# A chain of casting and adding GpSimd transfers ahead of a GEGLU kernel, and in its down stage

## Chip, cores and metric

One core of one Trainium2 chip. The metric is device time in microseconds (us), from launch to end on that core. Every time below is such a time or a time inside one profiled execution, counted from its first instruction.

## What is computed

The reference, cut to what matters:

```python
def reference(x, w_gate, w_up, w_down):       # x (32, 32, 1024); w_gate, w_up (1024, 3584); w_down (3584, 1024); all bf16
    return (gelu_tanh(x @ w_gate) * (x @ w_up)) @ w_down
```

With the two leading axes of x taken together it is a feed-forward layer on N = 1024 rows: two products of 1024 x 1024 by 1024 x 3584, a gated product of the two, and a product of 1024 x 3584 by 3584 x 1024.

## The kernel before

**Two stages.** The gate/up stage makes `hT`, the transposed gated product (28 blocks of 128 features, 1024 columns, bf16). The down stage multiplies it by w_down. Both use a seven-product scheme for two-by-two blocks in place of eight block products: sums and differences of operand blocks are formed first, products of these are made, and the results are combined. The sums are held in `S` (20 slots of 128 x 512, `F32R`) and `T` (eight units of 2 x 4 x 128 per partition, `F32R`); the down stage sees the same memory of `T` as 16 slots, `T2r`.

**Start.** The first columns of x come in through two plain loads into `xn` (a part of `hT`), one on SP's queue and one on ACT's. PE transposes them with the identity `ident`, which GpSimd (POOL) makes with a `memset` and an `affine_select`. Ahead of that PE runs eight warm-up matmuls on a constant. The rest of x comes through transposing transfers on SP's queue. The weight blocks of the first pairs are loaded by `load_quad`, on SP's queue and on ACT's, behind the two x loads.

**Gate/up.** Pairs p = 0 to 13 take feature blocks p and p + 14. `sums_w` makes the weight sums of a pair, some on DVE, some on POOL, one on ACT. The sums of x are in `S`; the last pair reads slots 12 to 15 in its product 3 and slots 16 to 19 in its product 4.

**Down.** `sweep` runs the products in the order 1, 2, 7, 5, 6, 3, 4. K is cut into NK = 14 blocks for each half. For products 7, 5 and 6 the first operand is made by `prep7`, `prep5` and `prep6`, two blocks of k at a time, into slots of `S` by

```python
s_at = lambda b, k: 2 * ((b * 7 + k // 2) % 10) + k % 2
hs = lambda b, k: S[:, s_at(b, k):s_at(b, k) + 2, :]
```

with b = 0 for product 7, 1 for product 5, 2 for product 6. So product 5 uses slots 14, 16, 18, 0, 2, 4, 6 (each with its neighbour) for k = 0, 2, ..., 12, and the last four pairs are those that product 7 read for k = 0, 2, 4, 6. `prep6` reads what `prep5` made. In `sweep` the first `EDGE` = 4 blocks of k run for three of the four row tiles and then for the fourth; the middle blocks run k by k over all four; the last four blocks run tile by tile.

**Order.** `_Program.add` records every operation with its engine and, from the memory cells that it reads and writes, the operations that it has to wait for; `after` adds more of these. `finish` sorts each engine's operations by a due time `at` and then by the order of recording; PE keeps the order of recording. `at` sorts only: no operation waits for it. `emit` issues each engine's list in order, with a wait on a semaphore ahead of an operation where one is needed, so an operation that waits holds up everything behind it on its engine, transfers included. All operations are issued in `emit`, so nearly all of them have one line in the profile, L117.

Of the kernel before, what the change touches and what calls it, by code (L numbers as in the profile page):

```python
# [6 lines left out]
P = 128  # L7
BF16 = mybir.dt.bfloat16
FP32 = mybir.dt.float32
F32R = mybir.dt.float32r  # L10
ACTF = mybir.ActivationFunctionType
ALU = mybir.AluOpType
# [111 lines left out]
def bass_standalone__geglu_ffn__sampling_kernel(  # L124
# [15 lines left out]
    x_r = xf.rearrange("(tc p) d -> p tc d", p=P)  # L140
    w_r = [w.rearrange("(dk p) f -> p dk f", p=P) for w in (w_gate, w_up)]
    wd_r = w_down.rearrange("(m p) d -> p m d", p=P)

    pr = _Program()

    with ExitStack() as es:
        def sb(name, shape, dtype):
            return es.enter_context(nc.sbuf_tensor(name, shape, dtype))

        hT = sb("hT", [P, FM, N], BF16)  # L150
        arena = sb("arena", [P, 28672], BF16)
        S = sb("S", [P, 20, 512], F32R)
        T = sb("T", [P, 8, 2, 4, P], F32R)
# [12 lines left out]
        xn = hT[:, FM - 1, :].rearrange("p (t c) -> p t c", c=2 * P)  # L166
        Sf = S[:, :, :].bitcast(FP32)
# [15 lines left out]
        def tt(out, a, b, op, at, eng="dve", after=()):  # L183
            return pr.add(eng, "tensor_tensor", out, a, b, op, at=at, after=after)
# [4 lines left out]
        def dma(eng, out, a, at, name, after=()):  # L189
            return pr.add(eng, "dma_start", out, a, at=at, dma=name, after=after)  # L190

        GELU, COPY = ACTF.Gelu_apprx_tanh, ACTF.Copy
        ADD, SUB, MUL = ALU.add, ALU.subtract, ALU.mult


        one = nc.const_aps.tensor(1.0, [P, 512], BF16)
        pr.add("pool", "memset", ident[:, :], 0.0)
        pr.add("pool", "affine_select", ident[:, :], ident[:, :], [[-1, P]], ALU.not_equal, 1.0,
# [3 lines left out]

        NX = 2
        for i, eng in enumerate(("sp", "act")):
            dma(eng, xn[:, 2 * i:2 * i + 2, :], x_r[:, 2 * i:2 * i + 2, 0:NX * P], 0, f"xn{i}")

        def load_quad(eng, q, j, k0, k1, at=0, after=()):
            dma(eng, quad[q][:, j, k0:k1, :], w_r[j][:, k0:k1, 4 * q * P:4 * (q + 1) * P], at, f"w{q}_{j}_{k0}", after)
# [81 lines left out]
        for m in (0, 2):  # L290
            at = 21.9 + 2.59 * m
# [76 lines left out]
        for p in range(8, EARLY):  # L368
            at = 18.9 + (p - 4) * 3.46
            g = (2, 0)[p - 8]  # L370
            u = g + 1
# [21 lines left out]
        for p in range(NP):  # L393
            t0 = T0[p]
            short, last = p < EARLY, p == NP - 1
# [9 lines left out]
            at = lambda s: t0 + s * SLOT  # L405
# [27 lines left out]
            o = 4 if short else 7.8 if last else 5.9  # L433
# [58 lines left out]
        def hb(i, j, k):  # L492
            m = (KL if j == 0 else KR)[k]
            return hT[:, m:m + 2, i * 512:(i + 1) * 512]
# [5 lines left out]
        def wb(i, j, k): return wd[i][j][:, k:k + 2, :]  # L500
# [5 lines left out]
        hs = lambda b, k: S[:, s_at(b, k):s_at(b, k) + 2, :]  # L506
# [52 lines left out]
        clock = base + 1.5  # L559
        V = 1.22  # L560
# [3 lines left out]
            tt(ws(0, k), wb(1, 1, k), wb(0, 1, k), SUB, clock + V * (7 + k / 2))  # L564

        def prep5(k):
            tt(hs(1, k), hb(1, 0, k), hb(1, 1, k), ADD, clock + V * (14 + k))
            tt(ws(1, k), wb(0, 1, k), wb(0, 0, k), SUB, clock + V * (15 + k))

        def prep6(k):  # L570
# [23 lines left out]
        one_w = lambda b: (lambda k: T2r[:, t_at(b, k), :])  # L594
        sweep(7, PA, True, one_t(0), one_w(0), lambda t, at: act(p7[t], bank(PA[t]), COPY, at), prep7)
        sweep(5, PA, True, one_t(1), one_w(1), lambda t, at: act(p5[t], bank(PA[t]), COPY, at), prep5)
        sweep(6, PB, False, one_t(2), one_w(2), lambda t, at: act(bank(PA[t]), bank(PB[t]), COPY, at), prep6)
        for t in range(4):
# [48 lines left out]
```

## Time and profile before

| what | value |
|---|---|
| median of the runs shown | 271.56 us (271.51 and 271.62) |
| span of the profiled execution | 270.8 us; 0.7 to 0.8 us of a run's time lie around it |
| PE (matmuls) busy | 268.2 us, 99% |
| PEld (weight loads) busy | 192.6 us, 71% |
| DVE busy | 208.2 us, 77% |
| ACT busy | 136.1 us, 50% |
| POOL busy | 37.1 us, 14% |
| mean granted TensorE clock | 1.000 |
| first x loads issued | 0.73 and 0.74 us |
| products 7, 5 and 6 of the down stage | 202.1 to 240.4 us |

PE is TensorE's matmul, PEld its weight load, which overlaps with it; DVE is VectorE, ACT ScalarE, POOL GpSimd, SP SyncE. A queue such as SPq is where that engine issues transfers. A line of the timeline has a start, a duration, the engine, the operation with its output and input, and a count; the part in brackets is idle time before it and what ended it. The kernel before issues no transfer from POOL: all of its own go through SP's and ACT's queues.

### The profile page before, as it was taken

The page shows a single profiled execution, that of the slowest core. Times are in us where ns is not written, and L with a number is a line of the kernel's source. Part 1 is how long each engine was busy: PE and PEld are TensorE (multiplying, and loading weights), DVE is VectorE, ACT ScalarE, POOL GpSimd, SP SyncE. Part 2 cuts the span into 40 slices and gives each one's busy share as a digit, 9 for nine tenths or more (in the row PEclk, how much of TensorE's full clock was granted, in tenths as well). Part 3 has the DMA queues.
Part 4 walks back from the last instruction along what each step waited for, and adds up shares of the span by engine and source line. Part 5 has one row for each costly group of instructions (what it writes and reads, how often), then busy time and mean ns, then how long its engine had stood idle before and what let it go on. Part 6 is the DMA issues. An engine that isn't in the chain of part 4 may idle for free.

```text
span 270.8 us, 3333 instructions
## 1 busy us (share of the span) xinstructions
PE 268.2 (99%) x1206; PEld 192.6 (71%) x1206; DVE 208.2 (77%) x246; ACT 136.1 (50%) x221; POOL 37.1 (14%) x23
## 2 busy tenths in 40 slices
PE   8999999999999999999999999999999999999997
PEld 4444448888888888888776776674458888888884
DVE  1338998998899889988764739379976999999921
ACT  2339877566756675667455554531220305057452
POOL 1000003123302330233344160000000000000000
DMA  6999970050492002971900070294010000002102
GB/s 205 205 316 204 280 188 4 13 141 0 116 291 60 0 0 80 254 251 51 263 0 0 0 247 27 65 351 129 0 39 19 4 0 0 0 0 80 58 21 97
DMA packets 45024, 27.47 MB, mean 101 GB/s; under 512 B 8656, under 2 KB 45008, under 8 KB 45008
## 3 DMA queue, kind: packets, MB, share of 16 engines
q1 hardware_dynamic: 42496, 25.04, 34.0%
q10 hardware_dynamic: 2512, 2.23, 3.3%
q8 instruction: 9, 0.15, 0.2%
q14 instruction: 7, 0.06, 0.1%
HBM read 23.33 MB, written 2.10 MB: 94 GB/s over the span
## 4 chain that ended last, share of the span: by engine, by line
PE 99%; DVE 0%; issue 0%
PE ps L117 99%; DVE o L117 0%
## 5 line engine op out<-in xcount | busy, mean ns | idle before, releaser
L117 PE MATMUL ps<-S,T 128*128 128x512 f32 x560 | 129.2, 391 | 0.0
L117 PEld LDWEIGHTS ps<-S,T 128*128 128x128 f32 x560 | 105.2, 188 | 22.3
L117 ACT ACTIVATE tmp<-ps 128x512 f32<-128x512 f32 x64 | 38.0, 596 | 51.7 <-PE ps L117 51.5
L117 POOL TENSOR_TENSOR T<-arena 128x1024 fp32r<-128x1024 bf16 x17 | 36.4, 2153 | 124.5 <-PE ps L117 81.7
L117 PE MATMUL ps<-T,S 128*128 128x512 f32 x224 | 51.3, 390 | 0.0
L117 DVE TENSOR_TENSOR T<-arena,T 128x1024 fp32r<-128x1024 bf16 x42 | 51.0, 1220 | 0.2
L117 PEld LDWEIGHTS ps<-T,S 128*128 128x128 f32 x224 | 42.1, 188 | 8.8
L117 ACT ACTIVATE ps<-ps 128x512 f32<-128x512 f32 x44 | 25.6, 584 | 37.0 <-PE ps L117 37.0
L117 DVE TENSOR_TENSOR hT<-tmp,ps 128x512 bf16<-128x512 f32 x56 | 37.0, 684 | 8.7 <-PE ps L117 6.7
L117 PE MATMUL ps<-arena 128*128 128x512 bf16 x192 | 43.5, 385 | 0.1
L117 DVE TENSOR_TENSOR tmp<-ps,tmp 128x512 f32<-128x512 f32 x28 | 19.4, 692 | 23.5 <-PE ps L117 23.5
L117 PEld LDWEIGHTS ps<-arena 128*128 128x128 bf16 x192 | 18.5, 99 | 23.7 <-issue 2.4
L117 DVE TENSOR_TENSOR T<-arena 128x1024 fp32r<-128x1024 bf16 x25 | 30.0, 1222 | 4.4 <-PE ps L117 4.3
L117 DVE TENSOR_TENSOR ps<-ps,tmp 128x512 f32<-128x512 f32 x32 | 22.3, 696 | 3.0 <-PE ps L117 3.0
L117 PE MATMUL ps<-arena,hT 128*128 128x512 bf16 (+2 forms) x126 | 24.6, 356 | 0.0
L117 PEld LDWEIGHTS ps<-arena,hT 128*128 128x128 bf16 x126 | 11.7, 98 | 12.7 <-issue 0.5
L117 ACT ACTIVATE tmp<-tmp 128x512 f32<-128x512 f32 x28 | 17.6, 632 | 2.4 <-DVE tmp L117 2.1
L117 ACT ACTIVATE ps<-hT 128x512 f32<-128x512 f32 x22 | 13.0, 599 | 7.6 <-DVE hT L117 7.6
L117 DVE TENSOR_TENSOR S<-hT 128x1024 fp32r<-128x1024 bf16 x14 | 16.6, 1221 | 0.0
L117 ACT ACTIVATE T<-arena 128x1024 fp32r<-128x1024 bf16 x14 | 14.8, 1059 | 0.0
L117 ACT ACTIVATE hT<-ps 128x512 f32<-128x512 f32 x18 | 9.5, 602 | 7.0 <-PE ps L117 7.0
L117 PE MATMUL ps<-S 128*128 128x512 f32 x56 | 12.9, 389 | 0.0
(33 smaller groups left out, 94.4 us busy)
## 6 DMA issues: line engine op xcount, KB each, us to landing
arena<-in_w_down_dram SPq DMA_DIRECT2D x4, 1792.0 KB, 9.4
arena<-in_w_gate_dram SPq DMA_DIRECT2D x10, 512.0 KB, 4.8
arena<-in_w_up_dram SPq DMA_DIRECT2D x10, 512.0 KB, 5.9
out_dram<-arena SPq DMA_DIRECT2D x12, 128.0 KB, 1.7
arena<-in_w_up_dram ACTq DMA_DIRECT2D x6, 128.0 KB, 5.6
arena<-in_w_gate_dram SPq DMA_DIRECT2D x3, 256.0 KB, 6.3
arena<-in_w_up_dram SPq DMA_DIRECT2D x3, 256.0 KB, 6.5
arena<-in_w_gate_dram SPq DMA_DIRECT2D x4, 128.0 KB, 5.1
```

The costliest lines, as they stand in the source:

```text
L117: ins = name(eng, *args, **kw) if callable(name) else getattr(eng, name)(*args, **kw)
```

## The change

Ahead of everything else stands a chain of transfers. SP loads 1 MiB of w_gate into the first four blocks of `hT`. Then come 13 steps on POOL, 24 transfers in all. Some copy with a cast to float32 into parts of `S` and `T`, some add onto what is there (`accum_op`). Sources are w_gate and w_up in main memory, the loaded blocks of `hT`, and parts of `S`. Each step waits for every transfer of the step before it, and each transfer has a semaphore of its own. What the chain writes is overwritten later and enters no result. The transfers of the last step are `gate`, and the two x loads wait for it.

In the down stage `prep5` no longer adds two blocks of `hT` on DVE. A transfer from POOL copies the first block, cast, into the slots of `S`, and a second transfer adds the second block onto it. Their due times are earlier than that of the addition was.

```diff
+        last = [pr.add("sp", "dma_start", hT[:, 0:4, :], w_r[0][:, 0:4, 0:1024], dma="probe_in")]
+        serial = [0]
+
+        def probe(out, a, *groups, add=False, n=1):
+            made = []
+            for o, i in zip(out, a):
+                kw = dict(accum_op=ALU.add) if add else {}
+                made.append(pr.add("pool", "dma_start", o, i, dma=f"probe{serial[0]}", after=list(last), **kw))
+                serial[0] += 1
+            last[:] = made
+
+        tu = [T[:, 0, j] for j in range(2)]
+        probe(tu, [w_r[j][:, 0:4, 0:P] for j in range(2)])
+        probe(tu, [w_r[j][:, 4:8, 0:P] for j in range(2)], add=True)
+        probe([S[:, 0:4, :]], [w_r[0][:, 0:4, 0:512]])
+        probe([S[:, 0:4, :]], [w_r[0][:, 4:8, 0:512]], add=True)
+        probe([S[:, 4:8, :]], [hT[:, 0:4, 0:512]])
+        probe([S[:, 4:8, :]], [hT[:, 0:4, 512:1024]], add=True)
+        probe([S[:, 4:6, :]], [hT[:, 0:2, 512:1024]], add=True)
+        probe([S[:, 8:12, :]], [Sf[:, 0:4, :]])
+        probe([S[:, 8:12, :]], [Sf[:, 4:8, :]], add=True)
+        probe([S[:, 12:16, :]], [S[:, 0:4, :].bitcast(FP32)])
+        probe([T[:, u, j] for u in (1, 2) for j in range(2)], [hT[:, k:k + 4, a:a + P] for k in (0,) for a in (0, P, 256, 384)])
+        probe([T[:, u, j] for u in (1, 2) for j in range(2)], [hT[:, k:k + 4, a:a + P] for k in (0,) for a in (512, 640, 768, 896)], add=True)
+        probe([S[:, i, :] for i in range(4)], [hT[:, i, 0:512] for i in range(4)], add=True)
+        gate = list(last)
...
         for i, eng in enumerate(("sp", "act")):
-            dma(eng, xn[:, 2 * i:2 * i + 2, :], x_r[:, 2 * i:2 * i + 2, 0:NX * P], 0, f"xn{i}")
+            dma(eng, xn[:, 2 * i:2 * i + 2, :], x_r[:, 2 * i:2 * i + 2, 0:NX * P], 0, f"xn{i}", gate)
...
         def prep5(k):
-            tt(hs(1, k), hb(1, 0, k), hb(1, 1, k), ADD, clock + V * (14 + k))
+            at = clock + V * (7 + k)
+            pr.add("pool", "dma_start", hs(1, k), hb(1, 0, k), at=at, dma=f"h{k}")
+            pr.add("pool", "dma_start", hs(1, k), hb(1, 1, k), at=at + 2.5, dma=f"g{k}", accum_op=ALU.add)
             tt(ws(1, k), wb(0, 1, k), wb(0, 0, k), SUB, clock + V * (15 + k))
```

`hT` blocks, `S` slots and `T` units that the chain touches are written by the kernel itself before it reads them.

## The prediction

> **What bounds the kernel now.** I read the page's part 1 and part 4 first, then the stage table, then the start and the waits.
>
> ```profile
> span 270.8 us, 3333 instructions
> PE 268.2 (99%) x1206; PEld 192.6 (71%) x1206; DVE 208.2 (77%) x246; ACT 136.1 (50%) x221; POOL 37.1 (14%) x23
> ...
> PE 99%; DVE 0%; issue 0%
> ```
>
> PE is busy for 268.2 of 270.8 us and the chain that ended last is PE throughout. Work taken from another engine is worth nothing unless PE waits for it; whatever holds PE up is paid one for one. The stage table (width; PE busy, PEld, DVE, ACT, POOL; clock; DMA) says the same of the stages that the change touches:
>
> ```profile
> core 0: us, PE busy (x) PEld busy (x) DVE busy (x) ACT busy (x) POOL busy (x), PEclk, DMA share, GB/s
> 202.00:214.80 12.80, 12.80 (x59) 10.55 (x57) 9.05 (x8) 2.31 (x4) 0.00 (x0) 1.00 0.03 11
> 214.80:227.60 12.80, 12.80 (x58) 10.62 (x57) 12.80 (x13) 2.48 (x5) 0.00 (x0) 1.00 0.01 1
> ```
>
> These are products 7 and 5 of the down stage. PE has no idle time in either, DVE is full in the second, POOL and the DMA engines stand almost empty. The start, from the timeline:
>
> ```profile
> 0.73 0.49 ACTq L117 DMA_DIRECT2D hT<-in_x_dram  x1
> 0.74 0.46 SPq L117 DMA_DIRECT2D hT<-in_x_dram  x1
> 0.77 2.93 PE L117 MATMUL ps<-const-bfloat16-1.0 128*128 128x512 bf16 x8 [0.77 <-PEq L632]
> 3.50 1.06 PE L117 MATMUL ps<-ident,hT 128*128 128x128 bf16 x8
> 6.67 3.55 PEld L117 LDWEIGHTS ps<-arena 128*128 128x128 bf16 x17 [0.25 <-issue]
> ```
>
> Both queues begin with an x load; all weight loads stand behind it. The eight warm-up matmuls need no data, the eight transposes at 3.50 do. So PE has 2.9 us of work that depends on no load, and no more.
>
> **Part 1, the chain ahead.** It adds 1 SP load and 24 GpSimd transfers in 13 steps, each step waiting for all of the step before. The last step is the gate of both x loads. These are first on SP and on ACT, so everything behind them on the two queues waits as well: all weight loads, the x transposes, and on ACT the table load and every activation. The price is therefore the chain's full length G, nearly one for one. The identity (0.20 and 0.29 us on POOL) is now queued behind the last issues of the chain; it is covered by the landing of those transfers and by the 2.77 us from the x issue (0.73) to the first transpose (3.50), and uncovered it would cost 0.5 us.
>
> The trace has no GpSimd transfer, no cast and no accumulation, so G is bounded from the nearest rows, which are of the SP and ACT queues:
>
> ```profile
> arena<-in_w_down_dram SPq DMA_DIRECT2D x4, 1792.0 KB, 9.4
> ...
> hT<-in_x_dram SPq DMA_DIRECT2D x1, 128.0 KB, 2.5
> ...
> out_dram<-o SPq DMA_DIRECT2D x1, 32.0 KB, 1.4
> ```
>
> (issues: size of one, us from issue to landing) and the groups:
>
> ```profile
> L117 POOL TENSOR_TENSOR T<-arena 128x1024 fp32r<-128x1024 bf16 x17 | 36.4, 2153 | 124.5 <-PE ps L117 81.7
> ```
>
> Bytes. Plain steps (1, 3, 5, 8, 10, 11) write 0.5+1+1+1+1+1 = 5.5 MiB = 5.77 MB at four bytes an element. Accumulating steps (2, 4, 6, 7, 9, 12, 13) write 6 MiB. I count them by what must be read, source and old destination: 0.75+1.5+1.5+0.75+2+1.5+1.5 = 9.5 MiB = 9.96 MB; the cheap end counts 6.29 MB, as if they were plain. Rate: in the window 120 to 200 us the load queue took this:
>
> ```profile
> q1 hardware_dynamic: 9762, 7.76, 31.9%
> ```
>
> 31.9% of 80 us is 25.5 us of all engines; 7.76 MB by that is 304 GB/s. The ends are 351 GB/s (the best 40th of the page) and 195 GB/s (the mean of the first 12 us, with its short runs and queueing).
>
> Completion, once per step: 1.4 us, the landing of the smallest transfer (32 KB), with 2.5 us, the 128 KB x load, as the dear end. Issue, per transfer: 0.49 us on ACT's queue at one end, one POOL instruction of 2.15 us at the other; I take 1.0, the geometric mean (√(0.49·2.15) = 1.03), because descriptors are written by an engine that runs its work slower than the two queues do. At the cheap end issues are wholly hidden by running transfers, zero.
>
> - Issues: 24 × 1.0 = 24.0 us (0 to 51.6).
> - Completions: 13 × 1.4 = 18.2 (to 13 × 2.5 = 32.5).
> - Plain bytes: 5.77/0.304 = 19.0; accumulated: 9.96/0.304 = 32.8. Together 51.8 (12.06/0.351 = 34.4 to 15.73/0.195 = 80.7).
> - SP's first load, 1 MiB: 1.4 + 1.05/0.304 = 4.8 (4.4 to 7.9).
>
> G = 98.8 us, ends 57.0 and 172.7.
>
> The Trainium skill, "DMA: Bandwidth & Descriptors", section on the anatomy of a GpSimd DMA, gives about 2.0 us fixed plus bytes at 436 GB/s for one such transfer. No row here shows a GpSimd transfer; by that fit, once per step, the chain would be an estimated 13 × 2.0 + 12.06/0.436 = 54 us and its time about 331 us. [...]
>
> **Part 2, the cold start.** After the warm-ups PE now idles through G. In the trace the first matmuls follow each other at 0.42 to 0.43 us until 6.67, which is 5.9 us after the first warm-up, and from there 17 weight loads take 3.55 us, 0.209 each (the granted clock column reads 1.00 all along, so the spacing is what I use). Before, 3.17 us of the slow pace fell after the first transpose; with the warm-ups long past it can be 5.9, 2.7 us more at half pace: 1.4 us lost (0 if the loads were the limit anyway). I take 1.4. The Trainium skill, "TensorE: Matmul & The Clock Gate", Part 1, has the array return to half clock after an idle window of some 3.4 us and leave it after about as long a busy one; by that the loss would be nearer 0.3 us.
>
> **Part 3, the down stage.** Removed: seven DVE adds (`S<-hT` of `prep5`), 1.22 us each, 8.5 us of DVE. Worth 0: PE has no idle time from 202 to 240 us, so nothing waited for them. The other DVE operations of the stage come earlier and meet buffers still read by PE. Added: 14 GpSimd transfers, 256 KiB read and 512 KiB written each, ordered h0 h2 g0 h4 g2 h6 g4 h8 g6 h10 g8 h12 g10 g12 (h casts, g adds, g waits for its h). POOL's last instruction of before ends at 162.4, so nothing else is queued there. h0, h2, h4 need slots of S last read at some 179 to 181 and are through by 202. h6 needs slot 0, which product 7 has read by 205.8 (16 of its matmuls of 0.2266 us from 202.1); h8 also 205.8, h10 207.5, h12 209.3. By the rows above h takes 1.0+1.4+0.52/0.304 = 4.1 us, g 1.0+1.4+0.79/0.304 = 5.0, one issue after another at 1.0. Then: h6 205.8, g4 206.8, h8 207.8, g6 209.9, h10 210.9, g8 211.9, h12 212.9, g10 215.0, g12 217.0, landing 222.0. Product 5 wants slot k=12 first at 214.8 + 42 × 0.2266 = 224.3, k=6 at 220.2 (there by 214.9). Slack 2.3 us: cost 0. At the dear end (issue 2.15, h 7.3, g 8.7) the same chain lands at 235.6: PE stalls 11.3 us, and DVE, whose `S<-S,hT` of product 6 read these sums, waits with it.
>
> The Trainium skill, "SBUF — State Buffer", summary of rules, speaks against this part: a GpSimd DMA should not be hidden under DVE work, since its descriptors starve while DVE holds the port they share. DVE is full here (12.80 of 12.80 us), but with two-input adds, which the same page infers to leave descriptor writing alone; no run here shows either. If each of the last four issues waited out one DVE add, the estimated loss would be 4 × 1.22 − 2.3 = 2.6 us.
>
> **Sum.** 98.8 + 1.4 + 0 = 100.2 on a span of 270.8: 371.0. The median shown, 271.56, is 0.76 above that span, so **372 us**.
>
> **Rivals.** (a) *Cheap chain*: issues hide under transfers and an accumulation costs what a copy does. For it: the DMA engines are otherwise idle. 57.0 more: 328; were only source bytes to count (7.6 MB at 351 GB/s, 21.7), G = 44.3 and the time 316. (b) *Dear chain*: per-descriptor work on POOL, or slow accumulation, decides. For it: POOL needs 2.15 us where DVE needs 1.22 for an operation of one size, and the chain has steps of 2,048 runs. 172.7 + 1.4: 446, with the down stall 457. (c) *The sums of product 5 come late* with an ordinary chain: slack is only 2.3 us, stall up to 11.3: 383. Against it: slots 14 to 18 are filled 20 us early. (d) *No change*: the chain is covered, because PE's first 2.9 us need no load. That decides up to G of 5.4 us, 2% of 271.6, which is about what a measurement of this kernel can tell from no change. Thirteen steps would have to take 0.4 us each, under a third of the quickest landing (1.4): time about 272.
>
> **Chances.** Forecast (around 340 to 415) 0.60, (a) 0.17, (b) 0.16, (c) 0.055, (d) 0.015. The range reaches from the cheap end of the bounds, 328, to the dear one with its stall, 457; about 2 in 10 lie outside. Faster by over 2% needs a gain that no row offers: 0.005. Within 2%: (d), 0.01. Slower: 0.985.
>
> **What would show it.** The first x issue at about 99.5 us instead of 0.73; PE idle between 3.7 and some 102; the rest of the timeline like before, shifted; a GpSimd DMA queue with 12.06 MB written ahead of the first x load and 14 × 0.52 = 7.3 MB in the down stage; product 5 without PE idle time. Right: PE busy still about 268 to 270 us. Wrong: x issues that start before the chain ends; a chain under 57 or over 173 us (then a row stood for the wrong thing); PE waiting within product 5 (Part 3 wrong); or a busy PE that grows by more than 3 us (Part 2 wrong).

## The result, and the profile after

The changed kernel takes 358.68 us (358.29 and 359.07) against 271.56 before: ratio 1.3207, 95% interval 1.3168 to 1.3245. The forecast was 372, with a range of 328 to 457. The direction and the mechanism held; the size was 87 us instead of 100. In every run on record that has both, the time lies 1.25 to 1.59 us above the span; the median before lies only 0.76 us above the span of its profile, so that profile is of an execution some 0.5 to 0.8 us slower than the two shown, and differences of spans come out a little too small.

The page of the changed kernel, parts 1 and 4:

```profile
span 357.0 us, 3389 instructions
PE 269.8 (76%) x1197; PEld 192.7 (54%) x1206; DVE 200.7 (56%) x239; ACT 136.2 (38%) x221; POOL 74.2 (21%) x61
...
PE 75%; DMA 21%; POOL 2%; issue 2%; DVE 0%; POOLq 0%; ACTq 0%
```

PE does the work it did (269.8 us busy against 268.2), in a span 86.2 us longer. The chain that ended last was PE alone; now 21% of it is DMA. The chain of waits in order of time (start, duration, what) shows how a step is made up:

```profile
17.38 5.28 DMA S<-in_w_gate_dram
22.66 0.28 issue
22.95 6.82 DMA S<-in_w_gate_dram
...
46.60 4.22 DMA S<-S
50.82 0.29 issue
51.11 6.95 DMA S<-S
...
355.11 0.29 DVE o L117
```

The four transfers are steps 3, 4, 8 and 9, each of 1 MiB written: 4.2 to 5.3 us for a copy, 6.8 to 7.0 for an addition, 0.28 or 0.29 between a landing and the next issue. The last line ends the kernel. The gate opens at 85.09 (timeline):

```profile
85.09 0.47 ACTq L117 DMA_DIRECT2D hT<-in_x_dram  x1
...
87.60 1.28 PE L117 MATMUL ps<-ident,hT 128*128 128x128 bf16 x8 [83.89 <-DMA hT<-in_x_dram]
...
93.97 8.95 PEld L117 LDWEIGHTS ps<-arena 128*128 128x128 bf16 x42 [0.25 <-issue]
...
287.89 38.72 PE L117 MATMUL ps<-T,S 128*128 128x512 f32 x168
```

The same two points late in the profile of before, product 7 and the last DVE operation:

```profile
202.10 38.44 PE L117 MATMUL ps<-T,S 128*128 128x512 f32 x168
...
269.04 0.29 DVE L117 CAST o<-ps 128x128 bf16<-128x128 f32 x1 [3.29 <-PE ps L117]
```

Set against before (transposes at 3.50, quick weight loads from 6.67, and these two), the loss divides by subtraction. The transposes start 84.10 us later: the chain. Product 7 starts at 287.89, 85.79 later: 1.69 more for the colder start. The last DVE operation is at 355.11, 86.07 later: 0.28 more in the down stage. There PE's waits have one new line:

```profile
PEld ps L117 <- DMA S<-hT: 0.4, 1, 0.4
```

It falls at 310.45 us, after 98 matmuls from 287.89, so at product 5's k = 12, where the prediction put the least slack.

### The profile page after: what moved, and what is told of

Read it like the earlier page. It is cut to its first block, busy times and chain, and to the rows that moved or that the text cites. A ratio compares the mean times of both kernels' runs of the same rounds, so it can differ in the third digit from the quotient of the medians.

```text
span 357.0 us, 3389 instructions
## 1 busy us (share of the span) xinstructions
PE 269.8 (76%) x1197; PEld 192.7 (54%) x1206; DVE 200.7 (56%) x239; ACT 136.2 (38%) x221; POOL 74.2 (21%) x61
## 4 chain that ended last, share of the span: by engine, by line
PE 75%; DMA 21%; POOL 2%; issue 2%; DVE 0%; POOLq 0%; ACTq 0%
PE ps L117 75%; DMA S<-hT 6%; DMA S<-S 4%; DMA S<-in_w_gate_dram 3%; DMA T<-hT 3%; DMA T<-in_w_up_dram 2%; POOL T L117 2%; DMA hT<-in_w_gate_dram 1%; DMA hT<-in_x_dram 1%; POOL S L117 0%; DVE o L117 0%; POOLq L115 0%; ACTq L115 0%
## 5 line engine op out<-in xcount | busy, mean ns | idle before, releaser
L117 PE MATMUL ps<-ident,hT 128*128 128x128 bf16 x8 | 1.2, 307 | 84.0 <-DMA hT<-in_x_dram 83.9
L117 ACT ACTIVATE tmp<-ps 128x512 f32<-128x512 f32 x64 | 38.0, 595 | 52.0 <-PE ps L117 51.8
L117 DVE COPY arena<-ps 128x256 bf16<-128x256 bf16 x4 | 1.0, 291 | 88.2 <-PE ps L117 88.2
L117 POOL DMA_DIRECT2D S<-hT x21 | 20.4, 1159 | 65.0 <-PE ps L117 41.5
L117 PE MATMUL ps<-arena,hT 128*128 128x512 bf16 (+2 forms) x124 | 24.3, 355 | 0.1
```

Of the source, the lines that this page charges most:

```text
L117: ins = name(eng, *args, **kw) if callable(name) else getattr(eng, name)(*args, **kw)
```

## The experiments

**The two halves apart.** One kernel keeps the chain and gives product 5 its DVE additions back, one drops the chain and keeps the transfers.

```diff
 # chain_only, from the changed kernel
-            pr.add("pool", "dma_start", hs(1, k), hb(1, 0, k), at=at, dma=f"h{k}")
-            pr.add("pool", "dma_start", hs(1, k), hb(1, 1, k), at=at + 2.5, dma=f"g{k}", accum_op=ALU.add)
+            tt(hs(1, k), hb(1, 0, k), hb(1, 1, k), ADD, clock + V * (14 + k))
 # down_only: the kernel before, with the opposite edit
```

> The chain ahead of the x loads stays, product 5 gets its sums from DVE again. Theory (the chain's length and the colder start are nearly all of the loss, the down stage some 0.3 us): 358.7 - 0.3 = 358.4 us. Rival (the transfers of the down stage hold PE or DVE up more than the one wait of 0.4 us shows): 355 us or less.

> No chain; only product 5's sums come from GpSimd transfers. Theory: the freed 8.5 us of DVE are worth nothing, since PE has no idle time there; PE waits once, 0.4 us, for the last sum (k = 12) and loses about 0.3 us: 271.9 us. Rival 1 (freed DVE time is worth something): 270 us or less. Rival 2 (descriptors starve behind DVE's additions, and it was the shift that hid it): over 273 us.

Measured: the chain alone 357.11 us (ratio to before 1.3148, 1.3124 to 1.3172); the transfers alone 272.89 (1.0040, 1.0024 to 1.0056). So the chain is nearly everything, and the down stage costs some 1.3 us by these medians, more than the theory's 0.3. In the profile of the transfers alone PE stands longer at the same k:

```profile
201.30 22.58 PE L117 MATMUL ps<-T,S 128*128 128x512 f32 x98
224.59 16.16 PE L117 MATMUL ps<-T,S 128*128 128x512 f32 x70 [0.72 <-DMA S<-hT]
```

From product 7's first matmul to the last DVE operation this run takes 67.95 us (201.30 to 269.25), the kernel before 66.94, and the chain alone 66.94 too: 1.01 us lost, where the changed kernel lost 0.28. The seven operations that DVE no longer runs (8.5 us by their durations; its busy time falls from 208.2 to 200.7 us) bought nothing. The difference between chain alone and changed kernel, 1.6 us in the times, can't be given to the down stage: in the profile of the chain alone TensorE is quick 3.8 us after its first transpose, in that of the changed kernel 6.4 us, which at half pace is 1.3 us by itself.

**POOL's order, or full DMA engines?** If POOL's in-order waits made the last sum late, spreading copy and addition further apart would help; if the DMA engines were full, it would not.

```diff
 # down_spread, from down_only
-            pr.add("pool", "dma_start", hs(1, k), hb(1, 1, k), at=at + 2.5, dma=f"g{k}", accum_op=ALU.add)
+            pr.add("pool", "dma_start", hs(1, k), hb(1, 1, k), at=at + 5.0, dma=f"g{k}", accum_op=ALU.add)
```

> As the kernel with the down stage's transfers alone, but the adding transfer of a pair is ordered after the copies of the next two pairs instead of the next one (due time + 5.0 instead of + 2.5), so that POOL need not wait for a copy to land before it issues on. Theory (the last sum is late because POOL waits in order for the copies to land): the last sum lands some 3 us earlier, PE doesn't wait for it: 271.6 us, no wait of PE for these transfers in the trace. Rival (the transfers are late because the DMA engines are full): the last sum lands at the same time, the wait of 0.4 us stays: 271.9 us.

Measured: 273.32 us (1.0061, 1.0047 to 1.0075), and PE waits twice, 0.24 and 1.05 us, until 225.58. The theory is refuted. The rival fits better but missed too: it had the last sum land at the same time, for 271.9 us, and it landed 1 us later. The edit also does more than was meant. The addition for k = 2 now stands behind the copy for k = 6, which waits for product 7, so ten transfers instead of nine fall into the stretch that counts. The DMA queue from 204 to 226 us (packets, MB, share of 16 engines' time), first of the transfers alone, then of this kernel:

```profile
q0 software_dynamic: 2448, 4.72, 87.7%
```

```profile
q0 software_dynamic: 2720, 5.24, 97.2%
```

Bytes and share rise alike: more transfers in flight don't move more bytes in the engines' time; each one lands later (median 7.0 us instead of 4.9). But only the spread kernel keeps the engines full to the end. With the transfers alone the queue's share falls to 14.2% from 220 to 221 us and 11.0% from 221 to 222, around the issue of the last addition (220.14), for which POOL had waited 3.41 us for its copy's landing. So the late sum is made of both: a crowded queue, in which that copy took 6.8 us to land, and then an addition that can't begin before it.

**Fewer sums by transfer.** The next two kernels keep the mechanism and take DMA time away.

```diff
 # down_three (k < 6) and down_five (k < 10), from down_only
+            if k < 6:
                 pr.add("pool", "dma_start", hs(1, k), hb(1, 0, k), at=at, dma=f"h{k}")
                 pr.add("pool", "dma_start", hs(1, k), hb(1, 1, k), at=at + 2.5, dma=f"g{k}", accum_op=ALU.add)
+            else:
+                tt(hs(1, k), hb(1, 0, k), hb(1, 1, k), ADD, clock + V * (14 + k))
```

> No chain; GpSimd transfers make product 5's sums for k = 0, 2, 4 only (slots 14, 16, 18, free 20 us ahead), DVE adds the other four. Theory (all of the down stage's loss is that four copies and five additions share the DMA engines from 205 to 224 us and the last lands late): no wait of PE for these transfers, 271.6 us, the same as before within 0.3 us. Rival (DVE's 3.7 us of freed time is worth something): 270.5 us or less. Rival 2 (the transfers disturb PE or DVE otherwise, by their traffic): 272.5 us or more.

> As the last, with transfers for k = 0 to 8 and DVE adds for k = 10 and 12. Theory (DMA time of 1.5 us a copy and 2.6 an addition, one after another, from 205.4 us: two copies and three additions end at 216.2, some 1.4 us later they have landed, k = 8 is wanted at 222): no wait of PE, 271.6 us. Rival (POOL's waits in order decide): a wait for k = 8 of 0.5 us or more, 272.3 us.

Measured: 271.46 us (0.9998, 0.9988 to 1.0009) and 271.49 (0.9994, 0.9984 to 1.0004). Neither has a wait of PE for these transfers. Ten transfers that land in time cost nothing, and five DVE operations fewer (6.1 us by their durations, 5.6 of busy time) bring nothing, within the 0.4 us or less that these intervals leave open: both halves of "worth 0" are shown. In the second, POOL does wait in order for landings, harmlessly:

```profile
POOL S L117 <- DMA S<-hT: 3.0, 2, 2.0
```

**Double the price.** Each copy made twice, so that a pair is three transfers in a row.

```diff
 # down_double, from down_only
             pr.add("pool", "dma_start", hs(1, k), hb(1, 0, k), at=at, dma=f"h{k}")
+            pr.add("pool", "dma_start", hs(1, k), hb(1, 0, k), at=at + 0.01, dma=f"i{k}")
```

> As the kernel with the down stage's transfers alone, but each copy is made twice, so that a pair is three transfers one behind the other. Theory (POOL waits in order for landings, the last sum was 0.4 us late, and nothing else has slack to give): each of the last two pairs adds a landing of about 4 us, so that PE waits 5 to 10 us in product 5: 277 to 282 us. Rival (POOL's waits for free slots of S decide, not the landings): under 274 us.

Measured: 288.13 us (1.0615, 1.0594 to 1.0636), beyond the theory's 277 to 282. PE waits four times:

```profile
PE ps L117 <- DMA S<-hT: 11.2, 4, 4.7
```

After the 4.73 us wait at 228.15, eight matmuls take 3.47 us, 0.43 each, and the mean granted clock from 201 to 255 us is 0.91: the wait cost TensorE its quick pace as well, which I hadn't counted. From 205.7 to 238.2 us, while transfers still come, the queue's share is 83.9%, with slices of 0.8 us in which no byte moves; over the same part the transfers alone have 100.5% (205.4 to 224.6) and the spread kernel 106.3% (205.5 to 225.6; packets overlap, so the share can pass 100%). So landings in a row weigh more here, and bytes less. No run separates the two fully.

**What a step costs.** In place of the 13 steps, single transfers one after another.

```diff
 # ladder, from the changed kernel (the chain's steps replaced)
+        for add in (False, True):
+            probe([S[:, 0, 0:P]], [hT[:, 0, 0:P]], add=add)
+            probe([S[:, 0, :]], [hT[:, 0, 0:512]], add=add)
+            probe([S[:, 0:4, :]], [hT[:, 0:4, 0:512]], add=add)
+            probe([T[:, 0, 0]], [hT[:, 0:4, 0:P]], add=add)
+        for n in (1, 4):
+            probe([Sf[:, 4:4 + n, :]], [Sf[:, 0:n, :]])
+            sp_step(Sf[:, 8:8 + n, :], Sf[:, 0:n, :])
+        probe([Sf[:, 4:8, 0:P]], [Sf[:, 0:4, 0:P]])
+        sp_step(Sf[:, 8:12, 0:P], Sf[:, 0:4, 0:P])
```

> In place of the 13 steps a ladder of single transfers, one after another, each waiting for the one before: GpSimd copies with a cast of 128 x 128, 128 x 512, 128 x (4 x 512) and 128 x (4 x 128) elements, the same four as additions, and then float32 copies within S without a cast, 128 x 512, 128 x 2048 and 128 x (4 x 128), each once from GpSimd and once from SP. The time means nothing but the ladder's length; it is read from the trace. Theory (a step is about 2 us of issue and completion, and bytes): small copies about 2.5 us, 128 x (4 x 512) about 4.4 as a copy and 6.9 as an addition, so that the addition costs by its bytes and its small ones cost little more than small copies; the same copy from SP 0.5 to 1 us quicker. Rival (the issue on POOL decides, by the number of runs): 128 x (4 x 128) costs as much as 128 x (4 x 512), and small additions cost clearly more than small copies.

Its chain of waits, with the issue lines left out; the first eight are the copies and then the additions of 128 x 128, 128 x 512, 128 x (4 x 512) and 128 x (4 x 128) elements, the last two the same float32 copy from GpSimd and from SP:

```profile
6.46 1.96 DMA S<-hT
...
8.71 2.27 DMA S<-hT
...
11.27 4.51 DMA S<-hT
...
16.06 2.67 DMA T<-hT
...
19.03 2.27 DMA S<-hT
...
21.58 2.95 DMA S<-hT
...
24.82 6.84 DMA S<-hT
...
31.95 3.88 DMA T<-hT
...
41.04 4.58 DMA S<-S
...
45.63 4.54 DMA S<-S
```

Between 128 x 512 and 128 x (4 x 512), 0.75 MiB written, a copy grows by 2.24 us and an addition by 3.89: 2.99 and 5.19 us for a MiB. What is left is 1.5 us for a copy and 1.65 for an addition, issue and completion together; the smallest pair, 128 x 128, lies 0.25 and 0.3 us above these lines. So an addition costs by its bytes, as the theory had it. Shorter runs cost something, not all: 512 runs of 128 elements take 0.4 us more than 128 runs of 512 as a copy, 0.9 more as an addition. And the same copy from SP is not 0.5 to 1 us quicker: 4.54 against 4.58, and 2.32 against 2.29 for the small one. Only the lines left out differ, 0.28 or 0.29 us from a landing to GpSimd's next issue and 0.02 to SP's. The rival, issue by number of runs, falls: 128 x (4 x 128) costs 2.67 and 3.88 us, far from the 4.51 and 6.84 of 128 x (4 x 512).

**Additions made copies, and steps without their wait.**

```diff
 # plain_adds
-                kw = dict(accum_op=ALU.add) if add else {}
+                kw = {}
 # free_order (and last.extend(made), so that the gate is all 24)
-                made.append(pr.add("pool", "dma_start", o, i, dma=f"probe{serial[0]}", after=list(last), **kw))
+                made.append(pr.add("pool", "dma_start", o, i, dma=f"probe{serial[0]}", **kw))
```

> The changed kernel with the chain's seven accumulating steps made copies of the same shapes; the down stage is unchanged. Theory (an accumulation costs by what it moves: from pairs of steps in the trace 1.4 + 1.5 + 2.3 + 1.3 + 2.7 + 3.7 + 1.4 = 14.3 us more than copies): 344.4 us. The recorded prediction (accumulations read 9.96 MB where copies write 6.29, at 304 GB/s: 12.1 us): 346.6 us. Rival (steps are completion and issue, bytes hide): 357 us or more.

> The changed kernel without the wait of every step for the step before: a transfer waits only for those whose data it reads, adds to or overwrites; the x loads wait for all 24. Theory (the chain is mostly the DMA engines' time: 65.4% of the first 92 us is 60 us; the rest, some 18 us, is issue and completion): the chain can't get below 6 + 60 us, the time is 342 us, with DMA engines busy throughout. The recorded prediction (42 us of issues and completions that could overlap): 320 to 330 us. Rival (data dependences alone keep the order): 355 us or more.

Measured, one run each: 342.03 us and 339.47. The gate opens, in the first and in the second, at

```profile
70.07 0.38 SPq L117 DMA_DIRECT2D hT<-in_x_dram  x1
```

```profile
67.06 0.39 SPq L117 DMA_DIRECT2D hT<-in_x_dram  x1
```

In the first that is 70.07 instead of 85.09: accumulation costs 15.0 us of the chain, near the 14.3 read from the pairs of steps; the rest of the 16.7 us in the time is within what the start's pace varies. In the second it is 18.0 us earlier, close to the theory's floor of 66. That match is partly luck: the floor left the first load standing, and here the first copies start at 1.26 us instead of 6.33, beside it. Not these waits but the transfers' own time is the larger part, though data still hold some transfers back (POOL waits up to 7.91 us for a landing).

**The gate.** Two kernels let the x loads go without waiting; the second also makes the identity ahead of the chain.

```diff
 # ungated
-            dma(eng, xn[:, 2 * i:2 * i + 2, :], x_r[:, 2 * i:2 * i + 2, 0:NX * P], 0, f"xn{i}", gate)
+            dma(eng, xn[:, 2 * i:2 * i + 2, :], x_r[:, 2 * i:2 * i + 2, 0:NX * P], 0, f"xn{i}")
 # ungated_ident: as well, the memset and affine_select of ident moved ahead of the chain
```

> The changed kernel with the x loads no longer waiting for the chain. Theory (the identity for the transposes stands behind the chain in POOL's queue): x is there early, but PE can begin only after POOL's last issue and the identity, at 82.7 instead of 87.6 us: 353.7 us. Rival (the gate is the whole price): 275 us or less.

> The changed kernel with the x loads not waiting for the chain and the identity made ahead of it on POOL. Theory (the kernel itself writes blocks 0 to 3 of hT and S, which the chain reads and writes to its end, so DVE stops at the first of these writes, due at about 26 us, and PE soon after): the chain hides behind some 25 us of work and no more: 330 us, PE idle from about 30 to 88 us. Rival 1 (the gate and the identity are the whole price, the chain runs beside the kernel): 275 us or less. Rival 2 (the loads and the chain share the DMA engines, the start slows as much as is gained): 350 us or more.

Measured, one run each: 358.55 and 342.97 us. Without the gate PE does begin as soon as the identity is there, but that is at 88.65 instead of 82.7:

```profile
88.65 1.01 PE L117 MATMUL ps<-ident,hT 128*128 128x128 bf16 x8 [84.94 <-POOL ident L117]
```

The chain's last issue has moved from 78.46 to 84.23, since the x and weight loads now share the engines with its first steps (the first step's last transfer lands after 8.55 us instead of 3.38): 5.8 us given away for the 4.9 hoped for. With the identity first, PE works from 8.08 and stops where the theory said, because DVE may not write `hT` before the chain has read it:

```profile
DVE hT L117 <- DMA S<-hT: 64.7, 1, 64.7
...
PE ps L117 <- DVE hT L117: 61.4, 1, 61.4
```

It stops later than I expected (39.6 us) and starts again later (100.98), since the chain beside the weight loads issues its last step only at 92.35 and DVE then has a queue to work off. 16 us of 87 are hidden; the expectation of 330 missed both contention and that queue.

**The cold start.** 30 more matmuls that wait for the chain's second last step.

```diff
 # late_warm; before_last holds the transfers of the step before the gate
+        for i in range(30):
+            pr.add("pe", "matmul", ps[:, 3, 0:512], one[:, 0:P], one[:, 0:512], start=True, stop=True,
+                   skip_group_check=False, after=before_last if i == 0 else ())
```

> The changed kernel with 30 more matmuls of 512 columns on the constant, which wait for the second last step of the chain and so run in the last 9 us before the x loads land. Theory (1.4 us of the loss is a TensorE that has gone slow while the chain ran): first weight loads of real work at 0.21 us spacing instead of 0.43, time 358.7 - 1.4 = 357.3 us. Rival (the start is bound by the loads, whatever the pace of the matmuls): 358.7 us.

Measured: 355.15 us (1.3072, 1.3054 to 1.3089), 3.5 us less than the changed kernel. From the late warm-ups' timeline:

```profile
86.87 0.90 PE L117 MATMUL ps<-ident,hT 128*128 128x128 bf16 x8
...
88.36 3.13 PEld L117 LDWEIGHTS ps<-arena 128*128 128x128 bf16 x16 [0.77 <-DMA arena<-in_w_gate_dram]
```

The mechanism is right, its size isn't: the expectation set the changed kernel against the kernel before, which itself has five slow matmuls, and the matmuls added do away with all of them. In the profile of the changed kernel the slow weight loads of real work last from 88.93 to 93.97, twelve at 0.42 to 0.43 us where 0.21 is the quick pace: 2.5 us. The gate in this run opened 0.38 us earlier besides. PE then waits 0.60 us for a weight load, so the loads are the next limit. By the two profiles the gain is 3.09 us at the last DVE operation: 0.73 in the start of the transposes, 2.16 from there to product 7, which is the pace, and 0.20 in the down stage.

## Why the prediction was right, and by what it missed

- **What bounds the kernel** held: PE's time is unchanged, and what holds it up is paid one for one. DVE's freed time was worth nothing, shown by the kernels with three and five pairs and no chain.
- **Queues behind the gate** held: all of the start moved by 84.1 to 84.8 us, weight loads, x transposes and table load with it. The identity behind the chain was covered, as said; the kernel without the gate shows what it costs once it isn't.
- **The chain, 98.8 us, measured 84.4** (0.73 to 85.09). The term that failed is the issues: 24 × 1.0, added to 13 completions as if each transfer were issued with nothing else going on. By the ladder one step's issue and completion together are 1.5 to 1.65 us, with the 0.28 of the wait 1.8 to 1.93: 6 × 1.8 + 7 × 1.93 = 24.3 us. What is left over, 6.9 us, is put down to the eleven further transfers of the steps with two or four, 0.6 each; POOL's issues ahead of the last transfers of these steps hold 7.8 us of the chain of waits. That is 31.2 where the prediction had 24.0 + 18.2 = 42.2. Bytes: 5.5 × 2.99 + 6 × 5.19 = 47.6 where it had 51.8; counting an addition by what it must read came within 5% (31.1 against 32.8), partly by luck. Step 9 adds float32 and reads 2 MiB where steps 4 and 6 read 1.5, yet it took 6.95 us against 6.82 and 6.81: in these rows the price went by the bytes written. First load: 5.6 (5.28 and 0.3 to the first issue) against 4.8.
- **The skill's fit** ("DMA: Bandwidth & Descriptors", anatomy of a GpSimd DMA) gave 54 us. A single small copy takes 2.0 to 2.3 us, near its fixed part, though the line through two sizes leaves 1.5. Its rate doesn't carry over: 2.99 us for a MiB written is 351 GB/s, and 5.19 us, for an addition, is 202. The cast isn't the reason, since the float32 copies (2.29 us for 0.25 MiB, 4.58 for 1) take 3.05 us a MiB without one.
- **The cold start, 1.4 us, measured 1.69** in this profile. But the slow pace after the first transpose lasted 3.8, 4.6, 4.7, 4.9, 5.0 and 6.4 us in six kernels that start after a long idle time, so the term, set against the 3.17 us of the one profile of before, is 0.3 to 1.6 us by the run. The start without the chain varies too: from the first transpose to product 7 six profiles without it take 197.59 to 198.60 us (before is the longest), and these six take 199.02 to 200.29. The means are 1.6 us apart, near the 1.4 forecast. The kernel with the late warm-ups took 198.13. The skill's 3.4 us ("TensorE: Matmul & The Clock Gate", Part 1), which it gives for one busy window and calls run-variable, is below all of the six; by the prediction's own arithmetic it would make 0.1 us of loss against 3.17, not the 0.3 stated. Its fall back to half clock after an idle window fits: the eight warm-ups of 0.78 us left no quick pace 84 us later, and the thirty right ahead of the work did.
- **The down stage, 0, measured 0.3 to 1.3 us.** The place (k = 12 of product 5) was right, the landing of the last sum wasn't: 222.0 forecast, 224.55 in the kernel with the transfers alone. The step that failed gave each of several transfers in flight the full rate: the last copy had 4.1 us to land and took 6.8, so that the last addition was issued at 220.14 and not at 217.0. Four copies of 1.5 us and five additions of 2.6 us of DMA time are 19.0 us from 205.4: 224.4, but that sum meets the landing partly by luck, since the engines are nearly idle for 2 us of it. So rival (c) happened, in small.
- **Descriptors starved by DVE** ("SBUF — State Buffer", summary of rules): not seen. An addition of 128 x (2 x 512) takes POOL 1.19 us with DVE idle (in the chain, at 41.96) and 1.20 and 1.21 with DVE full of two-input additions. No run tried another DVE operation.
- The other rivals: neither end of the chain's bounds came near, and no part of the gate was hidden.

The 0.28 us of the changed kernel's profile is one draw of many. From product 7's first matmul to the last DVE operation eight profiles with all seven pairs by transfer, in the same order, take 67.02 to 68.43 us, that is 0.1 to 1.5 us more than the 66.94 of all four without a late sum (before, the chain alone, three and five pairs). Between the two profiles set side by side above, the landing of the last copy differs: POOL waits 2.00 us for it in the changed kernel and 3.41 with the transfers alone. What makes landings differ from one execution to the next stays open.

## What to carry to other kernels

A gate on the first load of a queue costs the whole of what it waits for; look for everything queued behind it, and for what stands behind the gating work on its own queue. Price a chain of transfers as one fixed time for each dependent step plus the bytes. Price transfers that overlap by the engines' time as well as by their lone latencies, and add the wait of one that needs another's landing. Moving work to DMA pays only where the engine relieved was the limit, and is free only where the landing has slack; here the additions of three or five of seven pairs fitted at no cost and no gain.

## What had not been expected

- In the ladder a copy issued from GpSimd landed as quickly as the same copy from SP (4.58 and 4.54 us for 1 MiB; 2.29 and 2.32 for 256 KiB).
- In the ladder an accumulating transfer took POOL 0.87 to 1.28 us to issue, a copy 0.56 to 0.76.
- In the kernel with each copy made twice, a PE wait of 4.7 us was followed by eight matmuls at half pace, so a late transfer cost more than the wait it showed.
